# A gated feed-forward kernel behind pooled attention: a new opening, a plain end, GpSimd set aside earlier, next operands split first

## The chip, the cores and the metric

The kernel runs on one core of a Trainium2 chip. TensorE (PE) multiplies matrices, VectorE (DVE), ScalarE (ACT) and GpSimd (POOL) work on tiles, and SyncE (SP) issues the DMAs. The metric is the device time of one execution in microseconds (us), the median of several.

## The reference, cut to what matters

```python
# q, k, v: batch 8, heads 8, seq 576, head_dim 64;  w_a, w_b: 512 x 1536;  w_out: 1536 x 512
k_p = k.reshape(B, H, 72, 8, D).mean(axis=3)      # keys and values pooled by 8
v_p = v.reshape(B, H, 72, 8, D).mean(axis=3)
scores = q @ k_p.T / sqrt(D)
attn = exp(scores - max);  attn = attn / (attn.sum(-1) + 1e-9)
x = (attn @ v_p)            # laid out as 4608 tokens x 512
out = ((x @ w_a) * (x @ w_b)) @ w_out
```

The feed-forward weights reach the chip as 64-bit words and are turned into float32 there.

## The kernel before, in words

The 4608 tokens are 36 chunks of 128; three chunks make a half (384 tokens), two halves a pair, and there are six pairs. Every product is kept near float32 accuracy by parts: an operand is split into a high part (an fp32r copy, made by ScalarE) and a low part (the rest, a subtraction on VectorE or GpSimd), and one product is three matmuls, high by high, high by low and low by high.

A chunk passes through `chunk` (L797): its queries are split (L828), the scores are made on TensorE (`psc`, L913), VectorE subtracts the greatest score (L846, L847), ScalarE takes exponentials (L946), VectorE sums and inverts (L952, L953), the weights are divided (L958), split into high and low part `pr` and `rem` (L970, L972, L281) and turned on TensorE against an identity (`ptr`, L996): four turns for the high part, four for the low part, two for a remainder. ScalarE copies the turned parts out of PSUM (L1003). When the three chunks of a half are turned, `values_of` multiplies them by the pooled values (`po`, L1045 to L1048), and ScalarE and VectorE split the result into the operand tiles `xB`, `xT` (L1061, L281).

The feed-forward part runs over items. Items 0 to 7 are plain (`normal`, L1209 to L1211): 0 and 1 take the first half of pair 0, items 2 to 5 both halves, 6 and 7 the second half. From pair 1 on an item (`block`, L1352 to L1354) makes the inner products of a block of w_a and w_b by a scheme of seven products on sums and differences. Inner products gather in four PSUM banks `psXA`, `psXB`, `psYA`, `psYB`; the a and b parts are multiplied into gates `h`, which are split into `hh`. `outer` (L1427 to L1429) multiplies gates by w_out and adds to `y` in SBUF through two banks `acc` (L1489, L1492); from pair 2 on `outer_block` (L1459 to L1461) does it with seven products too, for which the gates are first combined (L1267) and w_out's sums are loaded from DRAM.

The order of the instructions is written by a planner while the program is built (`Machine`, with a rank for every task and an assumed cost for every operation). Elementwise work marked `either` goes to VectorE or GpSimd, whichever is free first in that plan, until the item number reaches `ALONE`. Each engine then runs its list strictly in order. Six PSUM banks serve the attention part while `psum["opening"]` holds; with the first inner product `close_opening` takes all four product banks away from it and two are left. Tiles with one buffer (`qh`, `ql`, `pr`, `rem`) or two (`weights`) make a chunk wait for an earlier one.

Of the kernel before, what the change touches and what calls it, by code (L numbers as in the profile page):

```python
# [9 lines left out]
F32 = mybir.dt.float32  # L10
# [75 lines left out]
SPARE = 1  # L86

ALONE = 8
# [13 lines left out]
NSLOT = 15  # L102

# [140 lines left out]
def attn_moe_kernel(ctx: ExitStack, tc: tile.TileContext, q, k, v, vr, wa, wb, wo, out):  # L244
# [86 lines left out]
    for item in items:  # L331
        due_item.append(t)
        t += 27.0 if item[0] == "s" else 13.0 * len(item[1])
# [17 lines left out]
    psum = {"free": ["att0", "att1", "XA", "XB", "YA", "YB"], "att": {"att0", "att1"}, "opening": True}  # L351
# [6 lines left out]
    def take_bank(name):  # L358
        tag = psum["free"].pop(0)
        return ps.tile([P, 512], F32, tag=tag, name=name), tag  # L360

    def give_bank(tag):
        if tag in psum["att"] or psum["opening"]:
# [18 lines left out]
    rawt.update({f: first_raw[:, f] for f in range(3)})  # L382
    spare = {n: sb.tile([P, 1536], I32, tag=f"x{t}", name=f"words_{n}", bufs=1) for n, t in zip("abo", ("T1", "T2", "T3"))}
# [20 lines left out]
    def convert_weights(name):  # L404
# [8 lines left out]
        for f in range(2):  # L413
            start(due_f[f] + delay - 6, load_words(f))
# [79 lines left out]
    def sums_outer():  # L494

        for j in range(NJ):
# [5 lines left out]
            kept["outer", j] = dr.tile([P, 2, 7, 2, P], F32, name=f"kept_outer_{j}")  # L502
# [29 lines left out]
            slots.give("rawo", j)  # L532

# [263 lines left out]
    def chunk(i, ready):  # L797
# [11 lines left out]
        yield until(("scores", i - 1))  # L809

        gap = P // 2 if len(parts) > 1 else 0
        qh = sb.tile([P, NK, P + P // 2], F32R, tag="qh", name=f"qh_{i}", bufs=1)
        ql = sb.tile([P, NK, P + P // 2], F32R, tag="ql", name=f"ql_{i}", bufs=1)
# [20 lines left out]
        yield until(("probs", i - 2))  # L834
# [3 lines left out]
        wide = weights[i % 2]  # L838
        s = wide[:, :, :SP]
        top = sb.tile([P, H], F32, tag="m", name=f"m_{i}")  # L840
        z = sb.tile([P, H], F32, tag="z", name=f"z_{i}")
# [60 lines left out]
        if i < SUMMED:  # L902
            for g0 in range(0, NK, 2):
                yield until(*(("keys", b, g0) for b, _, _ in by_batch))
                yield bank_there
                pt, tag = take_bank(f"psc_{i}_{g0}")
# [49 lines left out]
        yield either(  # L956
            H * SP,
            lambda eng: eng.tensor_tensor(  # L958
                out=s[:n], in0=s[:n], in1=z[:n].unsqueeze(2).broadcast_to([n, H, SP]), op=ALU.mult
            ),  # L960
        )
        mark("pooled", i)

        yield until(("turned", i - 1))
        pr = sb.tile([P, 2, H, KM], F32R, tag="pr", name=f"pr_{i}", bufs=1)
# [3 lines left out]
        def high():  # L969
            nc.scalar.copy(pr[:n, 0], s[:n, :, :KM])  # L970
# [3 lines left out]
        yield on_act(H * KM + 2 * H * KR, high, 3)  # L974

        def rest(eng):
            low_part(eng, pr[:n, 1], s[:n, :, :KM], pr[:n, 0])
            low_part(eng, rem[:n, :, 1], sr, rem[:n, :, 0])

        yield either(H * SP, rest, 2)  # L980
# [4 lines left out]
        if c0 == 0:  # L985
            yield until(("valued", half - 1))
            both = sb.tile([P, 2, NK, HB], F32R, tag="turned", name=f"turned_{half}", bufs=1)
            turned[half] = both[:, 0], both[:, 1], sb.tile([P, NG, HB], F32R, tag="rest", name=f"rest_{half}", bufs=1)

# [17 lines left out]
        for x in range(3):  # L1007
            yield bank_there
            pt, tag = take_bank(f"ptr_{i}_{x}")
# [11 lines left out]
    def values_of(j, rank):  # L1021
# [46 lines left out]
        for g0 in range(0, NK, per):  # L1068
            yield bank_there
            po, tag = take_bank(f"po_{j}_{g0}")  # L1070
# [12 lines left out]
    def prepare(p):  # L1083
# [20 lines left out]
        start(rank, split("B11", b11))  # L1104
        start(rank, combine(b11, b12, b11, "T1", ("operand", p, "B11")))
        start(rank + 1, split("B21", b21))
        start(rank + 2, combine(t2, b22, b11, "T2", ("T1", p)))
        start(rank + 3, split("T2", t2, ("T2", p)))
        start(rank + 4, split("T1", b11, ("T2", p)))
        start(rank + 5, combine(b12, b22, b12, "T3", ("T1", p)))  # L1110
        start(rank + 6, split("T3", b12, ("T3", p)))
        start(rank + 7, split("B22", b22, ("T2", p), ("T3", p)))
        start(rank + 8, combine(b21, b21, t2, "T4", ("T2", p), ("operand", p, "B21")))
        start(rank + 9, split("T4", b21, ("T4", p)))
# [490 lines left out]
```

## Time and profile before

| | before |
|---|---|
| runs, us | 998.48, 998.95, 999.3 (median 998.95) |
| profiled execution, us | 998.71, of which the profiled span is 996.9 |
| TensorE busy in the span | 960.7 us, 96% |
| VectorE, ScalarE, GpSimd busy | 867.9, 580.6, 83.3 us |

The span runs from the first instruction to the last; 1.8 us of the execution's time lie around it. A matmul's busy time overlaps with its neighbours', so the pace of TensorE is read from the distance of starts.

### The profile page before, as it was taken

The page shows a single profiled execution, that of the slowest core. Times are in us where ns is not written, and L with a number is a line of the kernel's source. Part 1 is how long each engine was busy: PE and PEld are TensorE (multiplying, and loading weights), DVE is VectorE, ACT ScalarE, POOL GpSimd, SP SyncE. Part 2 cuts the span into 40 slices and gives each one's busy share as a digit, 9 for nine tenths or more (in the row PEclk, how much of TensorE's full clock was granted, in tenths as well). Part 3 has the DMA queues.
Part 4 walks back from the last instruction along what each step waited for, and adds up shares of the span by engine and source line. Part 5 has one row for each costly group of instructions (what it writes and reads, how often), then busy time and mean ns, then how long its engine had stood idle before and what let it go on. Part 6 is the DMA issues. An engine that isn't in the chain of part 4 may idle for free.

```text
span 996.9 us, 16951 instructions
## 1 busy us (share of the span) xinstructions
PE 960.7 (96%) x5776; PEld 948.7 (95%) x5776; DVE 867.9 (87%) x1750; ACT 580.6 (58%) x1584; POOL 83.3 (8%) x93
## 2 busy tenths in 40 slices
PE   4689999999999999999999999999999999999997
PEld 3589999999999999999999999999999999999996
DVE  7987897589899999989899988989989889967777
ACT  4789897547766656674454584555475554443221
POOL 4331333161000000000000000000000000000000
PEclk9989999999999999999999999999999999999999
DMA  9768865566967878978857796876777666787661
GB/s 306 244 227 274 298 204 172 176 219 224 328 232 251 304 252 301 337 265 300 296 205 244 252 344 225 282 249 199 271 280 276 229 223 222 270 315 242 230 204 64
DMA packets 88342, 250.16 MB, mean 251 GB/s; under 512 B 9856, under 2 KB 17536, under 8 KB 88256
## 3 DMA queue, kind: packets, MB, share of 16 engines
q1 hardware_dynamic: 88256, 249.08, 72.0%
q8 instruction: 46, 0.75, 0.3%
q14 instruction: 40, 0.33, 0.1%
HBM read 197.13 MB, written 51.90 MB: 250 GB/s over the span
## 4 chain that ended last, share of the span: by engine, by line
PE 89%; DVE 7%; ACT 1%; issue 1%; DVEq 0%; ACTq 0%
PE acc L1459 6%; PE acc L1461 6%; PE acc L1460 6%; PE psc L913 5%; PE psXB L1352 4%; PE psXA L1352 4%; PE psXA L1354 4%; PE psXB L1353 4%; PE psXB L1354 4%; PE psXA L1353 4%; PE psYA L1352 3%; PE psYB L1352 3%; PE psYA L1354 3%; PE psYA L1353 3%; PE psYB L1354 3%; PE psYB L1353 3%
## 5 line engine op out<-in xcount | busy, mean ns | idle before, releaser
L1492 DVE TENSOR_TENSOR y<-acc,y 128x384 f32<-128x384 f32 x304 | 164.9, 553 | 27.9 <-PE acc L1461 23.4
L1259 ACT CAST hh<-h 128x384 fp32r<-128x384 f32 x168 | 85.1, 516 | 90.7 <-DVE h L1397 48.7
L281 DVE TENSOR_TENSOR hh<-h,hh 128x384 fp32r<-128x384 f32 x212 | 114.7, 558 | 5.0 <-ACT hh L1306 2.3
L1459 PE MATMUL acc<-hh,wo 128*128 128x384 f32 x336 | 116.5, 347 | 1.2 <-DVE y L1492 1.0
L1460 PE MATMUL acc<-hh,wo 128*128 128x384 f32 x336 | 113.9, 339 | 1.6 <-DVE hh L281 1.6
L1461 PE MATMUL acc<-hh,wo 128*128 128x384 f32 x336 | 113.7, 338 | 0.0
L1379 ACT COPY h<-psXA 128x384 f32<-128x384 f32 x90 | 43.2, 480 | 80.1 <-PE psXA L1354 79.7
L875 ACT ACTIVATE weights<-psc,least 128x72 f32<-128x72 f32 x240 | 74.0, 332 | 20.2 <-DVE least L891 19.7
L913 PE MATMUL psc<-kdiag,qh 128*128 128x144 f32 x320 | 59.3, 286 | 11.8 <-ACT kdiag L653 10.7
L1459 PEld LDWEIGHTS acc<-hh,wo 128*128 128x128 f32 x336 | 63.4, 189 | 3.8 <-DVE y L1492 3.5
L913 PEld LDWEIGHTS psc<-kdiag,qh 128*128 128x128 f32 x320 | 54.4, 204 | 12.6 <-issue 8.3
L1460 PEld LDWEIGHTS acc<-hh,wo 128*128 128x128 f32 x336 | 63.7, 190 | 2.2 <-DVE hh L281 2.2
L1461 PEld LDWEIGHTS acc<-hh,wo 128*128 128x128 f32 x336 | 63.5, 189 | 0.0
L1267 DVE TENSOR_TENSOR h<-h,h 128x384 f32<-128x384 f32 x96 | 52.9, 551 | 0.6
L1003 ACT CAST turned<-ptr 128x512 fp32r<-128x512 f32 x72 | 40.4, 592 | 21.3 <-PE ptr L996 21.1
L875 ACT ACTIVATION_READ_ACCUMULATOR weights<-psc,least 128x1 f32 x240 | 51.9, 216 | 0.0
L1397 DVE TENSOR_TENSOR h<-h,h 128x384 f32<-128x384 f32 x90 | 49.6, 551 | 0.4
L1352 PE MATMUL psXB<-xT,load 128*128 128x384 f32 x144 | 48.7, 338 | 0.0
L1352 PE MATMUL psXA<-xT,load 128*128 128x384 f32 x144 | 48.6, 337 | 0.0
L1353 PE MATMUL psXB<-xT,load 128*128 128x384 f32 x144 | 48.4, 336 | 0.0
L1353 PE MATMUL psXA<-xT,load 128*128 128x384 f32 x144 | 48.4, 336 | 0.0
L1354 PE MATMUL psXB<-xT,load 128*128 128x384 f32 x144 | 48.3, 336 | 0.0
(294 smaller groups left out, 3048.5 us busy)
## 6 DMA issues: line engine op xcount, KB each, us to landing
load<-kept_S SPq DMA_DIRECT2D x96, 512.0 KB, 5.0
load<-kept SPq DMA_DIRECT2D x72, 512.0 KB, 5.7
wo<-kept_outer SPq DMA_DIRECT2D x48, 512.0 KB, 4.3
wo<-kept_outer SPq DMA_DIRECT2D x48, 384.0 KB, 4.1
kept_S<-sum SPq DMA_DIRECT2D x24, 512.0 KB, 2.9
kept_outer<-osum SPq DMA_DIRECT2D x36, 256.0 KB, 3.7
out<-y SPq DMA_DIRECT2D x48, 192.0 KB, 2.1
kept<-sum SPq DMA_DIRECT2D x18, 512.0 KB, 6.4
```

Source lines behind the costliest of these rows:

```text
L281: eng.tensor_tensor(out=lo, in0=src, in1=hi.bitcast(F32), op=ALU.subtract)
L875: nc.scalar.activation(s[:n, h], src[:, h - hs.start], AF.Exp, bias=least[:n, h:h + 1], scale=SCALE, accum_out=z[:n, h:h + 1],)
L913: nc.tensor.matmul(pt[:n, j * hk:(j + 1) * hk], qq[:, g, cs], kd[:, g, w].rearrange("p e s -> p (e s)"), start=(x == 0), stop=(x == len(to ...
L1259: yield on_act(HB, lambda: nc.scalar.copy(e[:, 0], gf[item, src]))
L1267: yield either(HB, lambda eng: eng.tensor_tensor(out=t, in0=ta, in1=tb, op=ALU.subtract))
L1352: nc.tensor.matmul(pt, w[:, 0, mat, c], xo[:, 0, kk], start=(opens and kk == 0), stop=False, **more)
L1353: nc.tensor.matmul(pt, w[:, 0, mat, c], xo[:, 1, kk], start=False, stop=False, **more)
L1354: nc.tensor.matmul(pt, w[:, 1, mat, c], xo[:, 0, kk], start=False, stop=(kk == 1), **more)
L1459: nc.tensor.matmul(pt, w[:, 0], e[:, 0], start=opens, stop=False, **more)
L1460: nc.tensor.matmul(pt, w[:, 0], e[:, 1], start=False, stop=False, **more)
L1461: nc.tensor.matmul(pt, w[:, 1], e[:, 0], start=False, stop=True, **more)
L1492: yield on_dve(HB, lambda: nc.vector.tensor_tensor(out=acc[at], in0=pt, in1=acc[at], op=ALU.add))
```

## The change

Opening: the queries of chunk 1 get a tile of their own (`early_q`), chunk 2 gets a third `weights` tile, and the two of them no longer wait for the chunk before. For the first six chunks (`WHOLE`) the divided weights stay float32 in `pr` and are turned once, four turns instead of eight; high and low part are made from the turned result by ScalarE and VectorE. The four product banks are taken from the attention part one by one (`close`), and items 0 and 1 use the X banks alone. The first weight words are loaded at an earlier rank (`WORDS_RANK`), the first two items are due 6 us sooner, and chunks of pair 1 may not start before item 2.

End: the outer products of the last item are plain (`outer_last`): sixteen products in place of fourteen, from the gates themselves, without combining them; the results gather in eight banks. One more block of w_out is prepared for it (`left_plain`).

GpSimd: `ALONE` goes from 8 to 4. Next operands: in `prepare` the splits of a pair's operands get the rank -999.5.

```diff
-ALONE = 8
+SPLIT_RANK = -999.5
+ALONE = 4
...
+SOONER = 6.0
+WHOLE = PER_HALF * 2
+WORDS_RANK = 34.0
+WORDS_FIRST = 1
...
-        due_item.append(t)
+        due_item.append(t - (SOONER if len(due_item) < LEAD else 0.0))
...
-    def close_opening():
-        psum["opening"] = False
-        for tag in readable:
-            readable[tag] = tag in psum["free"]
-        psum["free"] = [x for x in psum["free"] if x in psum["att"]]
+    def close(tag):
+        psum["open"].remove(tag)
+        readable[tag] = tag in psum["free"]
+        if readable[tag]:
+            psum["free"].remove(tag)
...
+    early_x = sb.tile([P, 2, NK, P + P // 2], F32R, tag="xB22", name="early_q", bufs=1)
+    third = sb.tile([P, H, SP + 1], F32, tag="xT4", name="weights_2", bufs=1)
...
-            start(due_f[f] + delay - 6, load_words(f))
+            start(WORDS_RANK if f < WORDS_FIRST and name != "o" else due_f[f] + delay - 6, load_words(f))
...
-        yield until(("scores", i - 1))
+        yield until(("scores", i - 2 if 0 < i < 3 else i - 1))
...
-        yield until(("probs", i - 2))
+        if i != 2:
+            yield until(("probs", i - 2))
...
-        wide = weights[i % 2]
+        wide = third if i == 2 else weights[i % 2]
...
+        if whole:
+            yield until(("turned", i - 1))
+            pr = sb.tile([P, H, KM], F32, tag="pr", name=f"pr_{i}", bufs=1)
+            def divide_both(eng):
+                divide(eng, s[:n, :, KM:], s[:n, :, KM:])
+                divide(eng, pr[:n], s[:n, :, :KM])
+            yield either(H * SP, divide_both, 2)
...
+        def turn_whole(pt):
+            for g in range(NK):
+                src = pr[:n, 2 * g:2 * g + 2, :].rearrange("p a s -> p (a s)")
+                nc.tensor.transpose(pt[:, g * P:g * P + n], src, ident[:n, :n].bitcast(F32))
+        def take_whole(pt, tag):
+            yield m.SETTLE
+            src = pt.rearrange("p (g s) -> p g s", g=NK)[:, :, :n]
+            hi, lo = (turned[half][x][:, :, c0:c0 + n] for x in range(2))
+            yield on_act(NK * n, lambda: nc.scalar.copy(hi, src))
+            yield on_dve(NK * n, lambda: low_part(nc.vector, lo, src, hi))
...
-        start(rank + 3, split("T2", t2, ("T2", p)))
+        start(SPLIT_RANK, split("T2", t2, ("T2", p)))
...
-                    bank = ("X", "Y")[u if len(us) > 1 else y] + "AB"[mat]
+                    bank = ("X", "Y")[u if len(us) > 1 else y if u else 0] + "AB"[mat]
...
+        if item == items[-1]:
+            for name, what in (("B11", "C11"), ("B22", "C22"), ("B12", "C12"), ("B21", "C21")):
+                start(rank, split(name, what, what))
+                start(rank, leave(what, "split " + name))
+            return
...
+    def outer_last(item, x0):
+        a11, a12, a21, a22 = 0, 5, 7, 6
+        first = [("C11", a11), ("C21", a21)]
+        steps = [(0, *x, "B11", True, False) for x in first]
+        for c in range(2):
+            for what, l1, l2 in (("C12", a11, a12), ("C22", a21, a22)):
+                steps += [(c, what, l1, "B12", True, False), (c, what, l2, "B22", False, True)]
+        steps += [(1, *x, "B11", True, False) for x in first]
+        steps += [(c, what, left, "B21", False, True) for c in range(2) for what, left in (("C11", a12), ("C21", a22))]
...
+            def products():
+                nc.tensor.matmul(pt, w[:, 0], e[:, 0], start=opens, stop=False)
+                nc.tensor.matmul(pt, w[:, 0], e[:, 1], start=False, stop=False)
+                nc.tensor.matmul(pt, w[:, 1], e[:, 0], start=False, stop=ends)
...
+            if p == 1:
+                x = max(x, LEAD)
```

TensorE, from the turning of chunk 2 to the first values product. Before (`ptr` turns, `psc` scores, `po` values product):

```order
L996 MATMUL ptr_0_343<-ident,pr_321 128x128 x4
L996 MATMUL ptr_1_349<-ident,pr_321 128x128 x4
L996 MATMUL ptr_2_354<-ident,rem_322 96x128 x2
L913 MATMUL psc_0_365<-kdiag_72,qh_336 128x144 x2
L913 MATMUL psc_0_365<-kdiag_72,ql_337 128x144
L913 MATMUL psc_0_365<-kdiag_72,qh_336 128x144 x2
L913 MATMUL psc_0_365<-kdiag_72,ql_337 128x144
L913 MATMUL psc_2_375<-kdiag_72,qh_336 128x144 x2
L913 MATMUL psc_2_375<-kdiag_72,ql_337 128x144
L913 MATMUL psc_2_375<-kdiag_72,qh_336 128x144 x2
L913 MATMUL psc_2_375<-kdiag_72,ql_337 128x144
L1045 MATMUL po_0_386<-turned_229,vdiag_74 128x384
```

TensorE at the same place now, from the turning of chunk 0 (L1045 is the float32 turn):

```order
L1045 MATMUL ptr_0_259<-ident,pr_230 128x128 x4
L1063 MATMUL ptr_2_268<-ident,rem_243 96x128 x2
L1045 MATMUL ptr_0_289<-ident,pr_271 128x128 x4
L1063 MATMUL ptr_2_298<-ident,rem_278 96x128 x2
L1045 MATMUL ptr_0_320<-ident,pr_301 128x128 x4
L1063 MATMUL ptr_2_329<-ident,rem_308 96x128 x2
L1117 MATMUL po_0_344<-turned_257,vdiag_74 128x384
L1118 MATMUL po_0_344<-turned_257,vdiag_74 128x384
```

The scores of chunk 3 stood ahead of the values product and now stand behind the first twenty-four inner products; the scores of chunks 0 to 2 all stand ahead of the first turn, and four turns of each chunk are gone.

VectorE, from the row after chunk 2's inverse sum to the division of its weights (`weights_81`, `pr_301`), as it stands now:

```order
L287 TENSOR_TENSOR rem_243<-weights_77,rem_243 128x2x32
L287 TENSOR_TENSOR own_21_252<-raw_first,own_21_252 128x512
L768 TENSOR_REDUCE vp_171<-early_9_95 96x64
L998 TENSOR_TENSOR weights_78<-weights_78,z_152 128x8x8
L998 TENSOR_TENSOR pr_271<-weights_78,z_152 128x512
L768 TENSOR_REDUCE vp_171<-early_9_95 96x64
L287 TENSOR_TENSOR turned_257<-ptr_0_259,turned_257 128x4x128
L287 TENSOR_TENSOR rem_278<-weights_78,rem_278 128x2x32
L798 SCALAR_TENSOR_TENSOR kv_5_294<-vp_171,mask 96x256 x2
L998 TENSOR_TENSOR weights_81<-weights_81,z_212 128x8x8
L998 TENSOR_TENSOR pr_301<-weights_81,z_212 128x512
```

Before, one row (`vrem`) stood between that inverse and the division of chunk 2; the work of chunks 0 and 1 that now stands there came ahead of chunk 2's exponentials.

TensorE at the end of the program, from the middle of the last inner product (`psXB`) on. Before:

```order
L1354 MATMUL psXB_5_0_11564<-xT_5_10552,load_466_11557 128x384
L1352 MATMUL psXB_5_0_11564<-xT_5_10552,load_466_11557 128x384
L1353 MATMUL psXB_5_0_11564<-xT_5_10552,load_466_11557 128x384
L1354 MATMUL psXB_5_0_11564<-xT_5_10552,load_466_11557 128x384
L1459 MATMUL acc_5_0_1_11771<-hh_187_11758,wo_469_11655 128x384
L1460 MATMUL acc_5_0_1_11771<-hh_187_11758,wo_469_11655 128x384
L1461 MATMUL acc_5_0_1_11771<-hh_187_11758,wo_469_11655 128x384
L1459 MATMUL acc_5_0_0_11743<-hh_190_11768,wo_468_11654 128x384
```

Now:

```order
L1433 MATMUL psXB_5_0_11538<-xT_5_10486,load_480_11531 128x384
L1591 MATMUL acc_5_0_C_11733<-hh_481_11601,wo_482_11628 128x384
L1592 MATMUL acc_5_0_C_11733<-hh_481_11601,wo_482_11628 128x384
L1593 MATMUL acc_5_0_C_11733<-hh_481_11601,wo_482_11628 128x384
L1591 MATMUL acc_5_0_C_11737<-hh_481_11601,wo_483_11629 128x384
L1592 MATMUL acc_5_0_C_11737<-hh_481_11601,wo_483_11629 128x384
L1593 MATMUL acc_5_0_C_11737<-hh_481_11601,wo_483_11629 128x384
L1591 MATMUL acc_5_0_C_11741<-hh_174_11726,wo_482_11628 128x384
```

All 48 matmuls of the last outer products now stand behind the last inner product; before, 3 of 42 stood ahead of it. The first six work on a gate (`hh_481`) that is made two products earlier.

## Rows read from the trace of the kernel before

**Rows 1.** The page: TensorE's busy time, and its tenths in 40 slices.

```profile
PE 960.7 (96%) x5776; PEld 948.7 (95%) x5776; DVE 867.9 (87%) x1750; ACT 580.6 (58%) x1584; POOL 83.3 (8%) x93
PE   4689999999999999999999999999999999999997
```

**Rows 2.** Windows: length, busy us of each engine, granted clock, DMA share, GB/s.

```profile
30.00:40.00 10.00, 4.86 (x23) 4.27 (x24) 9.29 (x14) 8.29 (x19) 4.20 (x5) 1.00 0.76 254
120.00:160.00 40.00, 40.00 (x249) 39.84 (x248) 33.89 (x65) 38.45 (x115) 13.79 (x14) 1.00 0.53 178
130.00:230.00 100.00, 100.00 (x608) 99.66 (x606) 75.52 (x140) 67.25 (x199) 40.39 (x38) 1.00 0.54 184
300.00:500.00 200.00, 199.18 (x1222) 197.80 (x1221) 186.13 (x395) 124.01 (x363) 0.57 (x2) 1.00 0.81 287
980.00:997.00 17.00, 10.82 (x41) 7.45 (x39) 11.24 (x22) 2.00 (x4) 0.00 (x0) 0.90 0.26 93
```

**Rows 3.** Timeline of TensorE's opening: start, us, line, tiles, [idle before].

```profile
13.55 0.41 PE L913 MATMUL psc<-kdiag,ql 128*128 128x144 f32 x1
...
33.71 0.75 PE L996 MATMUL ptr<-ident,pr 128*128 128x128 f32 x4 [4.75 <-ACT pr L970]
...
39.76 0.61 PE L1045 MATMUL po<-turned,vdiag 128*128 128x384 f32 x1
...
45.02 0.45 PE L1209 MATMUL psXA<-xB,own 128*128 128x384 f32 x1 [1.28 <-DVE xB L281]
...
47.23 0.34 PE L913 MATMUL psc<-kdiag,qh 128*128 128x144 f32 x2
...
49.87 0.38 PE L1209 MATMUL psXB<-xB,own 128*128 128x384 f32 x1
50.09 0.34 PE L1210 MATMUL psXB<-xB,own 128*128 128x384 f32 x1
...
52.02 0.80 PE L996 MATMUL ptr<-ident,pr 128*128 128x128 f32 x8
...
60.31 0.51 PE L996 MATMUL ptr<-ident,pr 128*128 128x128 f32 x4 [1.67 <-DVE weights L847]
...
64.29 0.42 PE L996 MATMUL ptr<-ident,rem 128*96 128x128 f32 x2 [0.77 <-ACT turned L1003]
...
64.95 0.52 PE L1428 MATMUL acc_n<-hh,wo 128*128 128x384 f32 x1
65.27 0.52 PE L1429 MATMUL acc_n<-hh,wo 128*128 128x384 f32 x1
```

**Rows 4.** Timeline of the other engines in the opening.

```profile
27.84 0.68 ACT L946 ACTIVATE weights<-weights 128x576 f32<-128x576 f32 x1
...
35.67 1.28 POOL L281 TENSOR_TENSOR own<-raw_first,own 128x512 fp32r<-128x512 f32 x1 [0.48 <-ACT own L454]
...
36.14 1.35 DVE L281 TENSOR_TENSOR ql<-q,qh 128x512 fp32r<-128x512 f32 x1 [0.56 <-ACT qh L828]
37.42 0.68 DVE L441 SCALAR_TENSOR_TENSOR raw_first<-raw_first,words_a 128x512 int32<-128x512 int32 x1
```

**Rows 5.** Groups by shape, 130 to 230 us: instructions, busy us, mean ns.

```profile
L281 POOL TENSOR_TENSOR own<-raw,own 128x512 fp32r<-128x512 f32 x5 | 6.7, 1332 | 27.2 <-ACT own L488 16.0 <-ACT own L454 9.1 <-PE acc_n L1429 2.2
L281 DVE TENSOR_TENSOR own<-raw,own 128x512 fp32r<-128x512 f32 x11 | 9.9, 911 | 0.0
```

**Rows 6.** TensorE's waits from 250 to 400 us: what waited for what, us, times, longest.

```profile
PE po L1045 <- ACT weights L875: 0.8, 1, 0.8
```

**Rows 7.** Timeline of the end.

```profile
979.92 0.34 PE L1354 MATMUL psXB<-xT,load 128*128 128x384 f32 x1
980.10 0.38 PE L1459 MATMUL acc<-hh,wo 128*128 128x384 f32 x1
...
993.28 0.34 PE L1461 MATMUL acc<-hh,wo 128*128 128x384 f32 x1
993.66 0.56 DVE L1492 TENSOR_TENSOR y<-acc,y 128x384 f32<-128x384 f32 x1 [0.21 <-PE acc L1461]
```

More of the change, by code (lines that the diff above doesn't have):

```diff
@@ L356, in bank_there, with later_bank_there, take_bank @@
         return bool(psum["free"])
-    def take_bank(name):
-        tag = psum["free"].pop(0)
+    def later_bank_there():
+        return any(x not in ("XA", "XB") for x in psum["free"])
+    def take_bank(name, later=False):
+        tag = [x for x in psum["free"] if not later or x not in ("XA", "XB")][0]
+        psum["free"].remove(tag)
         return ps.tile([P, 512], F32, tag=tag, name=name), tag
     def give_bank(tag):
-        if tag in psum["att"] or psum["opening"]:
+        if tag in psum["att"] or tag in psum["open"]:
             psum["free"].append(tag)
@@ L532, in sums_outer, with left_plain @@
             slots.give("rawo", j)
+    def left_plain():
+        j = NJ - 1
+        yield until(("kept", "outer", j, 3))
+        yield lambda: at_item[0] >= items.index(("s", NPAIR - 2, 0)) and slots.can("osum")()
+        e = slots.take("osum", (j, 7), [P, 2, 2, 2, P], F32R)[:, :, :1]
+        yield tmps.can("o")
+        w = tmps.take("o", "left", tmp_shape, F32)
+        yield transfer(w, kept["raw o", 2 * j], 1 << 18)
+        by = w[:, 256:].rearrange("p (o c s) -> p c o s", o=1, c=2)
+        yield on_act(256, lambda: [nc.scalar.copy(e[:, c, :, 0], by[:, c]) for c in range(2)], 2)
+        yield either(256, lambda eng: [low_part(eng, e[:, c, :, 1], by[:, c], e[:, c, :, 0]) for c in range(2)], 2)
+        tmps.give("o", "left")
+        for c in range(2):
+            dst = kept["outer", j][:, c, 7:8].rearrange("p o l s -> p (o l s)")
+            yield transfer(dst, e[:, c].rearrange("p o l s -> p (o l s)").bitcast(F32), 1 << 17)
+        mark("kept", "outer", j, 7)
+        slots.give("osum", (j, 7))
     def spare_for(kind):
@@ L1005, in take_turned @@
             mark("placed", i, x)
-        for x in range(3):
-            yield bank_there
-            pt, tag = take_bank(f"ptr_{i}_{x}")
+        if whole:
+            yield later_bank_there if i >= PER_HALF else bank_there
+            pt, tag = take_bank(f"ptr_{i}_0", i >= PER_HALF)
+            yield on_pe(NK * 0.21, lambda: turn_whole(pt))
+            start(rank, take_whole(pt, tag))
+        for x in range(2 if whole else 0, 3):
+            yield later_bank_there if i >= PER_HALF else bank_there
+            pt, tag = take_bank(f"ptr_{i}_{x}", i >= PER_HALF)
             yield on_pe(mms(NK if x < 2 else NG, n), lambda: turn(x, pt))
@@ L1131, in attn_moe_kernel @@
         if kind == "s" and item[1] >= 2:
-            order_o += [(j, c, x) for c in range(2) for x in range(2)]
+            order_o += [(j, c, x, 4 if item == items[-1] else 4 - x) for c in range(2) for x in range(2)]
         else:
@@ L1177, in there @@
         def there():
-            if psum["opening"]:
-                close_opening()
+            if bank in psum["open"]:
+                close(bank)
             return readable[bank]
@@ L1405, in outer @@
             kind, p, j = item
+            if item == items[-1]:
+                yield from outer_last(item, x)
+                continue
             if kind == "s" and p >= 2:
@@ L1439, in outer @@
                         opens, closes = j == LEAD, j == LEAD - 1
-                    start(TOP + 1, taken_outer(p if kind == "s" else 0, half, c, bank, pt, opens, closes))
+                    start(TOP + 1, taken_outer(p if kind == "s" else 0, half, c, (acc_free, bank), pt, opens, closes))
     def outer_block(item, x0):
@@ L1496, in taken_outer @@
             yield MARGIN
-        acc_free[bank] = True
+        if isinstance(bank, str):
+            give_bank(bank)
+        else:
+            bank[0][bank[1]] = True
         if closes:
@@ L1548, in attn_moe_kernel @@
         start(SUMS_RANK, sums_outer())
+        start(SUMS_RANK, left_plain())
         start(1e3, load_parts())
```

108 lines of the change are left out of this document (74 added, 34 removed).

## The prediction, made before the changed kernel was run

> **What bounds the kernel now.** I read the page first. TensorE is busy in 96% of the span, and its tenths show where it is not: the first four slices and the last [rows 1]. The windows say the same of the middle: from 300 to 500 us TensorE lacks 0.8 us of 200, with VectorE at 93% (186.1 of 200) [rows 2]. So the middle is TensorE's own work, and a change can win only at both ends, or lose in the middle by making TensorE wait. The timelines of the ends came next, as idle time and pace. The pace: twelve 384-column matmuls run from 49.87 to 52.02, so 0.18 us each (the last eleven 0.175); twenty-four 144-column ones from 47.23 to 49.87, so 0.11 each [rows 3]. The spacing of 0.32 us at 64.95 is TensorE at its lower clock, 1.2 GHz, after the gaps ahead of it; 0.175 is 2.4 GHz.
>
> In the opening the first inner product starts at 45.02 us, though only 94 matmuls stand ahead of it: 48 of 144 columns, 30 turns and 16 of 384, about 11 us of work at the fast pace. After it TensorE still idles in four gaps from 60.31 to 64.29 (1.67 the first, 0.77 the last, 3.6 together) and then runs nine wide matmuls and eight of half the width at the low clock [rows 3], which costs 9 x 0.145 + 8 x 0.11 = 2.2 us. What holds it is a chain through VectorE, which is busy in 9.29 of 10 us there [rows 2].
>
> At the end the last inner product ends near 980.1 and the last matmul starts at 993.28 [rows 7]: 13.4 us for 39 matmuls that need 6.8, so 6.5 us are waits and slow clock (granted clock 0.90 in that window [rows 2]).
>
> **The opening, step by step.** Chunk 0's scores end at 13.96 in the old kernel (13.55 + 0.41 [rows 3]). Now chunks 1 and 2 need no tile of the chunk before, so their 24 matmuls follow at once; at the low clock 0.22 each, 5.3 us, to 19.3. VectorE's greatest and difference, and the older rows of its list, I put at 2.1 us: chunk 2's exponentials start near 21.4 and not at 27.84 [rows 4]. They take 0.68. Then VectorE has the sum, the inverse and the twelve instructions shown in the order: seven of 512 columns or so at 0.68 [rows 4] and seven small ones that I put at 0.27 each, 6.7 us, so chunk 2's division is done at 28.8; the old kernel turned that chunk at 33.71 [rows 3]. Four turns at the low clock, 0.75 for the old ones [rows 3], 1.5 if a float32 turn costs two of those; the copy behind four conversions on ScalarE about 2 us. The values product starts near 32.5 and not at 39.76, because chunk 3's scores no longer stand between. From there to the first inner product it was 5.3 us, on the same rows, and I keep that: 37.8, I take 38. That is 7.0 us earlier, of which chunk 3's 12 scores, done later now, take back 1.3: 5.7.
>
> After that start the new order has 72 inner products (12.7 us) with one chunk's scores between, ahead of the next turn, where the old one had gaps worth 3.6 + 2.2 = 5.8. The X banks alone serve them, so each must be read out before it opens again; I allow 2 us of such waits. Gain 3.8. Opening in all: 9.5 us. The bounds are 4 (only half of the chain shortens, the gaps move later) and 13 (nothing waits).
>
> Edits that I cost at nothing. The earlier weight words: two loads of 512 KB go ahead of batch 1's keys, which come about 4 us later at 254 GB/s [rows 2]; the next thing that needs those keys, chunk 4's scores, stands behind the 72 inner products. If that cover were gone it would cost those 4 us. The float32 turn: 24 of them replace 48, eight of which took 0.80 with the last one's end [rows 3]. No row has a float32 matmul. Between the same price each (0.10, a gain of 2.4 us) and two 384-column matmuls (0.35, a loss of 3.6) I take 0.20, the pair it replaces, the nearest row: nothing. The later chunks of pair 1 and the bank rule change what is ready, not how much is done.
>
> The Trainium skill, "FP8 and Floating Point Precision" (TensorE Precision Notes), says that true float32 goes through the array in four passes. By that a turn costs 0.40 and the sum would be 4.8 us higher; no row here shows it.
>
> **The end.** The last item no longer combines gates, and 48 matmuls replace 42. Three of the old ones ran before the inner product's end, so that end comes 0.5 earlier, at 979.6. 48 x 0.175 = 8.4. The first six work on a gate made two products earlier and cover 1.05 us of splitting; the next gate's low part stands behind the last product's VectorE row, and I allow 0.4. Last matmul done at 988.4 in place of 993.5: 5.1. Behind it one addition (0.56 [rows 7]) and a store as before; the eight stores now come closer together, 0.3. Gain 4.8, between 2 (half of the waits come back) and 6 (no wait, old tail).
>
> **GpSimd off from item 4, and the split rank.** From 130 to 230 us GpSimd runs 38 instructions, 40.4 us [rows 2]. At VectorE's price, 0.68 for 512 columns [rows 4] against 1.33 on GpSimd [rows 5], that is 20.6 us. VectorE gets some time back: its own 512-wide rows took 0.911 there and 0.68 alone, 11 times, 2.5 us [rows 5]. So 75.5 + 20.6 - 2.5 = 93.6 of 100 us, as from 300 to 500, where TensorE lost 0.8 in 200. I take a loss of 1.0. The bounds: a gain of 0.8, the longest wait that the middle now has [rows 6], and a loss of 20.6. The splits of the next operands move ahead of gates and additions in two engines that keep TensorE fed; the old middle has no wait at a change of pair, so I cost it at nothing, inside the same bounds.
>
> VectorE's 1.35 us at 36.14 stands beside GpSimd's 35.67 to 36.95, and the same width takes 0.68 alone [rows 4]. The Trainium skill, "SBUF — State Buffer" (Who interferes with whom), has a rule for it: the two share a port pair under an exclusive lock for the whole instruction. By that rule GpSimd's new work in the opening, chunk 1's low part and chunk 0's division, would hold VectorE up once each, 0.7 us a time, and the sum would be 1.3 higher; the trace agrees with the lock.
>
> **The sum.** Against the profiled execution: 998.7 - 9.5 - 4.8 + 1.0 = 985.4. Its time is 0.2 under the median of the runs, so 985.6; I say 985.5.
>
> **The rivals.** *ScalarE keeps the pace.* From 120 to 160 us it is busy in 38.45 of 40 us [rows 2]; a TensorE that is 9.5 us ahead wants its rows sooner. The change takes from ScalarE one 512-wide copy and one 512-wide read per chunk, 12 x 0.5 = 6 us for six chunks. If the lead shrinks to that, 3.5 us come back: 989. For it: that window. Against: the list was also idle early, and TensorE had no wait there.
>
> *The lead is lost wholly.* The float32 turning takes no wide subtraction from VectorE, it only moves it behind the turn, and VectorE is 93% busy. If its list is the bound all through the opening, the first inner product comes earlier but the gaps return behind it. Then only the end remains: 998.9 - 4.8 + 1.0 = 995.1. Against: the order has 72 inner products ready.
>
> *Slower: VectorE becomes the bound.* The place is 130 to 230 us, the price GpSimd's 20.6. It decides once VectorE's 24.5 idle us there cannot be used, because its rows come in bunches behind TensorE's banks: TensorE then waits for gates and additions. With both ends' gains the time is 998.9 - 14.3 + 20.6 = 1005. Against: 93% from 300 to 500 at hardly any cost.
>
> **How the numbers follow.** Forecast 0.62 (981 to 988.5); ScalarE 0.20 (987 to 993); lead lost 0.08 (993 to 997); slower 0.08 (1001 to 1008); the rest, 0.02, is an offset of gains and losses within 0.2%, about 2 us, which is what a measurement of this kernel can tell from no change. The range 980 to 993 leaves out the last three and the forecast's lower edge, under 2 in 10. Faster 0.90, same 0.02, slower 0.08.
>
> **What would show it.** Right: the first inner product at 38 +- 2 us, no gap over 1 us between it and 70 us and no low clock there; from the end of the last inner product to the last matmul's end under 9.5 us; TensorE short of less than 4 us from 100 to 970. Wrong: the first inner product after 41 us; gaps behind it that ScalarE or VectorE ends; waits for `h`, `hh` or `y` between 130 and 300; turns of chunks 0 to 5 well over 0.8 us for four at the fast clock.

## The result and the profile after

The changed kernel takes 981.4 us (median of 981.18, 981.36, 981.44 and 984.44) against 998.72 for the kernel before in the same comparison: ratio 0.9831, 95% interval 0.9813 to 0.9848. The forecast was 985.5 in 980 to 993. Executions of one kernel differ by up to 4.5 us, mostly with TensorE's granted clock: some have low stretches, at 1.2 GHz in place of 2.4, most often between 60 and 100 us (mean of an execution 0.991 to 1.000); where that matters, spans at a mean clock of 1.0 are compared, which is called equal clock below. The profiled execution of the changed kernel, 984.44 us, is the one of the four that has such stretches.

The page: busy time, and TensorE's tenths, to be read beside [rows 1].

```profile
PE 954.3 (97%) x5758; PEld 945.3 (96%) x5758; DVE 864.8 (88%) x1779; ACT 574.0 (58%) x1571; POOL 44.6 (5%) x60
PE   4799999999999999999999999999999999999998
```

Only the first two slices and the last are under nine tenths now; before, the first three and the last were. GpSimd lost 39 us of work, and VectorE is no busier than before (867.9 in [rows 1]). The windows, as in [rows 2]:

```profile
40.00:70.00 30.00, 28.10 (x182) 27.15 (x181) 28.30 (x58) 26.13 (x56) 11.04 (x12) 1.00 0.74 257
70.00:100.00 30.00, 28.12 (x169) 27.58 (x168) 24.26 (x50) 27.15 (x78) 5.31 (x5) 0.89 0.82 266
130.00:230.00 100.00, 100.00 (x603) 99.54 (x602) 84.48 (x175) 65.37 (x188) 0.56 (x2) 1.00 0.58 199
```

From 130 to 230 us VectorE is busy for 84.5 us. I had worked out 93.6 for it. The opening on the other engines, to be read beside [rows 4]:

```profile
21.08 0.68 ACT L984 ACTIVATE weights<-weights 128x576 f32<-128x576 f32 x1 [1.12 <-DVE weights L885]
...
27.84 0.67 DVE L998 TENSOR_TENSOR pr<-weights,z 128x512 f32<-128x512 f32 x1
...
32.74 0.68 DVE L287 TENSOR_TENSOR turned<-ptr,turned 128x512 fp32r<-128x512 f32 x1
```

These are chunk 2's exponentials, its division and the low part of its turned weights. TensorE's opening, beside [rows 3]:

```profile
28.57 1.12 PE L1045 MATMUL ptr<-ident,pr 128*128 128x128 f32 x4 [0.90 <-DVE pr L998]
...
32.23 0.69 PE L1117 MATMUL po<-turned,vdiag 128*128 128x384 f32 x1 [2.01 <-ACT turned L1051]
33.48 0.69 PE L1118 MATMUL po<-turned,vdiag 128*128 128x384 f32 x1 [0.56 <-DVE turned L287]
...
36.84 0.48 PE L1120 MATMUL po<-rest,vrem 96*128 96x384 f32 x1
...
39.38 0.44 PE L1283 MATMUL psXA<-xB,own 128*128 128x384 f32 x1 [1.36 <-DVE xB L287]
...
69.68 0.36 PE L1118 MATMUL po<-turned,vdiag 128*128 128x192 f32 x1 [1.46 <-DVE turned L287]
...
73.07 0.52 PE L1510 MATMUL acc_n<-hh,wo 128*128 128x384 f32 x1
73.39 0.52 PE L1511 MATMUL acc_n<-hh,wo 128*128 128x384 f32 x1
...
90.75 0.54 PE L1063 MATMUL ptr<-ident,pr 128*128 128x128 f32 x4 [1.53 <-ACT weights L913]
```

The row at 28.57 is the float32 turn of chunk 2, still at the low clock. The first inner product starts 5.6 us earlier than in [rows 3]. No wait over 0.1 us follows it up to 63 us; then the gaps are back, 1.46 and 1.53 us the longest, and the spacing of 0.32 at 73.07 is the low clock. The end, beside [rows 7]:

```profile
970.01 0.34 PE L1433 MATMUL psXB<-xT,load 128*128 128x384 f32 x1
970.19 0.33 PE L1591 MATMUL acc_C<-hh,wo 128*128 128x384 f32 x1
...
971.54 0.44 PE L1592 MATMUL acc_C<-hh,wo 128*128 128x384 f32 x1
...
978.69 0.34 PE L1593 MATMUL acc_C<-hh,wo 128*128 128x384 f32 x1
```

The 48 matmuls run through, with one hold of 0.11 us at 971.54. And TensorE's waits from 100 to 970 us (what waited for what: us in all, times, longest) are one row, where the kernel before had four, 1.9 us in all:

```profile
PE psXB L1431 <- DVE h L1464: 0.5, 2, 0.3
```

### The profile page after: what moved, and what is told of

The parts are those of the page before. It is cut to its first block, busy times and chain, and to the rows that moved or that the text cites. A ratio compares the mean times of both kernels' runs of the same rounds, so it can differ in the third digit from the quotient of the medians.

```text
span 982.6 us, 16941 instructions
## 1 busy us (share of the span) xinstructions
PE 954.3 (97%) x5758; PEld 945.3 (96%) x5758; DVE 864.8 (88%) x1779; ACT 574.0 (58%) x1571; POOL 44.6 (5%) x60
## 4 chain that ended last, share of the span: by engine, by line
PE 93%; DVE 4%; ACT 1%; issue 1%; DMA 1%; SPq 0%; POOL 0%; DVEq 0%; ACTq 0%
PE acc L1541 6%; PE acc L1543 6%; PE acc L1542 6%; PE psc L951 5%; PE psXB L1431 4%; PE psXB L1433 4%; PE psXA L1431 4%; PE psXB L1432 4%; PE psXA L1432 4%; PE psXA L1433 4%; PE psYB L1431 3%; PE psYA L1431 3%; PE psYB L1433 3%; PE psYA L1432 3%; PE psYA L1433 3%; PE psYB L1432 3%
## 5 line engine op out<-in xcount | busy, mean ns | idle before, releaser
L1619 DVE TENSOR_TENSOR y<-acc,y 128x384 f32<-128x384 f32 x290 | 157.1, 552 | 25.6 <-PE acc L1543 17.0
L1333 ACT CAST hh<-h 128x384 fp32r<-128x384 f32 x165 | 83.0, 516 | 78.9 <-DVE h L1476 41.8
L1541 PE MATMUL acc<-hh,wo 128*128 128x384 f32 x322 | 110.0, 342 | 0.0
L1542 PE MATMUL acc<-hh,wo 128*128 128x384 f32 x322 | 108.3, 336 | 0.0
L1543 PE MATMUL acc<-hh,wo 128*128 128x384 f32 x322 | 108.3, 336 | 0.0
L951 PE MATMUL psc<-kdiag,qh 128*128 128x144 f32 x312 | 55.4, 277 | 9.3 <-ACT kdiag L687 8.5
L951 PEld LDWEIGHTS psc<-kdiag,qh 128*128 128x128 f32 x312 | 51.7, 197 | 9.7 <-issue 8.0
L1542 PEld LDWEIGHTS acc<-hh,wo 128*128 128x128 f32 x322 | 60.5, 188 | 0.0
L1541 PEld LDWEIGHTS acc<-hh,wo 128*128 128x128 f32 x322 | 60.5, 188 | 0.0
L1543 PEld LDWEIGHTS acc<-hh,wo 128*128 128x128 f32 x322 | 60.4, 188 | 0.0
L1341 DVE TENSOR_TENSOR h<-h,h 128x384 f32<-128x384 f32 x92 | 50.5, 549 | 0.5
L1476 DVE TENSOR_TENSOR h<-h,h 128x384 f32<-128x384 f32 x90 | 49.4, 549 | 0.3
L1431 PE MATMUL psXA<-xT,load 128*128 128x384 f32 x144 | 48.7, 338 | 0.0
L1432 PE MATMUL psXA<-xT,load 128*128 128x384 f32 x144 | 48.4, 336 | 0.0
L1433 PE MATMUL psXA<-xT,load 128*128 128x384 f32 x144 | 48.3, 336 | 0.0
```

The source lines that it names most:

```text
L951: nc.tensor.matmul(pt[:n, j * hk:(j + 1) * hk], qq[:, g, cs], kd[:, g, w].rearrange("p e s -> p (e s)"), start=(x == 0), stop=(x == len(to ...
L1333: yield on_act(HB, lambda: nc.scalar.copy(e[:, 0], gf[item, src]))
L1341: yield either(HB, lambda eng: eng.tensor_tensor(out=t, in0=ta, in1=tb, op=ALU.subtract))
L1431: nc.tensor.matmul(pt, w[:, 0, mat, c], xo[:, 0, kk], start=(opens and kk == 0), stop=False, **more)
L1432: nc.tensor.matmul(pt, w[:, 0, mat, c], xo[:, 1, kk], start=False, stop=False, **more)
L1433: nc.tensor.matmul(pt, w[:, 1, mat, c], xo[:, 0, kk], start=False, stop=(kk == 1), **more)
```

## The experiments

Each was timed beside the kernel before, whose median was 999.0 to 999.3 in these comparisons.

### Does the sum divide as forecast? The opening alone, and the opening with the end

The opening alone: the changed kernel without `outer_last` and `left_plain`, with

```diff
-ALONE = 4
+ALONE = 8
-        start(SPLIT_RANK, split("B11", b11))
+        start(rank, split("B11", b11))
...
-            order_o += [(j, c, x, 4 if item == items[-1] else 4 - x) for c in range(2) for x in range(2)]
+            order_o += [(j, c, x, 4 - x) for c in range(2) for x in range(2)]
```

> The changed kernel's opening with the old end, the old ranks of the splits and GpSimd up to the eighth item. My prediction's term (9.5 us): 989.6. Theory A (the rest of the 17.3 us, when the end's 4.8 and 4.5 for the middle are taken away, is the opening's): 991. Theory B (an earlier opening runs into GpSimd's and the splits' waits in the middle, so that part of its gain is given back there): 993 to 996, with waits between 200 and 420 us of 4 us or more.

989.02 us, ratio 0.9894 (0.9881 to 0.9908): about 10 us, as forecast (9.5). Its windows behind the start of the inner products, and then the first of these windows of the kernel before:

```profile
40.00:70.00 30.00, 28.09 (x182) 27.15 (x181) 28.19 (x57) 26.17 (x56) 11.00 (x12) 1.00 0.74 255
70.00:100.00 30.00, 27.98 (x189) 27.43 (x189) 26.39 (x54) 29.35 (x84) 5.36 (x5) 1.00 0.87 283
```

```profile
40.00:70.00 30.00, 25.16 (x149) 24.08 (x149) 26.12 (x52) 23.98 (x58) 12.46 (x14) 0.89 0.61 198
```

The clock is full in both of its windows. In the kernel before a mean of 0.89 over 30 us is 3.3 us of full clock not granted; TensorE idles for part of that stretch, so its matmuls lose 2.5 to 3 us by it. So the middle edits are not needed for the opening's gain, and theory B (given back in the middle) fell: TensorE's waits from 100 to 970 us are 1.8 us here. Theory A, 991, was 2 us too high. Which of the opening's edits gave what is not shown: but for the turning, below, none was taken back by itself.

With the plain end added, the middle edits alone put back:

```diff
-ALONE = 4
+ALONE = 8
...
-        start(SPLIT_RANK, split("B11", b11))
+        start(rank, split("B11", b11))
```

> The changed kernel with both middle edits put back: GpSimd works up to the eighth item and the splits have their old ranks; the new opening and the plain end stay. Theory A (the two middle edits are worth the sum of what each cost when put back alone, 4.7 and about 3 us): 988 to 989. Theory B (each only moves a wait that the other creates or removes; the opening alone gave 989.0 and the end is worth 4.8 to 5): 984 to 985, so that both together are worth about 3. My prediction's term (a loss of 1.0): 980.4.

984.9 us, ratio 0.9857 (0.9844 to 0.9871). So the end is worth 4.1 on the opening, and the two middle edits together 3.5 more; at equal clock (spans 982.4 and 983.4 against 979.4 to 979.7) it is 3 to 4. That is theory B's number. My term for them was a loss of 1.0. TensorE's waits from 100 to 970 us here:

```profile
PE acc_s L1510 <- DVE hh L287: 0.8, 1, 0.8
PE ptr L1063 <- DVE rem L287: 0.6, 1, 0.6
PE psXA L1433 <- DVE sum L287: 0.4, 1, 0.4
```

### The end taken back

```diff
-            if item == items[-1]:
-                yield from outer_last(item, x)
-                continue
...
-        start(SUMS_RANK, left_plain())
```

> The changed kernel with the old end: the last item combines its gates again, 42 matmuls in place of 48. Theory A (the plain end's gain is the waits between the last inner product and the last matmul, worked out at 4.8 us): 986.2, and 13 to 14 us from the end of the last inner product to the last matmul's end. Theory B (the old end's waits came from the late state of VectorE in the old middle and are gone without the plain end too): 982 to 984.

988.91 us, ratio 0.9893 (0.9879 to 0.9907). Four of its five executions have the low stretch and one has not: that one takes 986.2, theory A's number, with a span of 984.4 us against 979.4 to 979.7, so the end is worth 4.8 at equal clock. The waits are those of the kernel before; first two of them here, then the longest of the kernel before:

```profile
972.79 0.44 PE L1534 MATMUL acc<-hh,wo 128*128 128x384 f32 x1 [1.44 <-DVE hh L287]
...
978.70 0.44 PE L1533 MATMUL acc<-hh,wo 128*128 128x384 f32 x1 [0.65 <-DVE y L1611]
```

```profile
981.91 0.44 PE L1460 MATMUL acc<-hh,wo 128*128 128x384 f32 x1 [1.44 <-DVE hh L281]
```

Theory B (the old end's waits go without the plain end too) fell.

### The middle edits, one at a time, on the changed kernel

GpSimd back to the eighth item:

```diff
-ALONE = 4
+ALONE = 8
```

> The changed kernel with one number put back: GpSimd works up to the eighth item again and not only up to the fourth. Theory A (what TensorE lacked between 200 and 970 us in the kernel before came from the pair GpSimd and VectorE holding each other up, and the early end of GpSimd's work took it away): about 985 us, 3 to 4.5 above the changed kernel's 981.4, and waits between 200 and 420 us of 3 us or more. Theory B (the earlier splits of the next operands took it away): 980.5 to 982.5. Theory C (my prediction's term: GpSimd's absence costs 1 us): 980.4.

986.4 us, ratio 0.9874 (0.9861 to 0.9888): 5.0 more. Its two longest waits from 100 to 970 us:

```profile
PE psYA L1283 <- ACT own L503: 1.0, 1, 1.0
PE psYA L1285 <- DVE own L287: 0.8, 1, 0.8
```

They come at 221 to 223 us, for weights that ScalarE and VectorE split late. With a third of 0.5 us for `y` they are 2.3 us, not theory A's 3 or more; all waits from 100 to 970 us are 2.8 us, against 0.5 in the changed kernel. So waits are about half of the 5.0, and the rest is not assigned to a row. VectorE's rows for them and for the sums of w_out by shape from 130 to 230 us (busy us, mean ns), with GpSimd at work:

```profile
L287 DVE TENSOR_TENSOR osum<-rawo,osum 128x256 fp32r<-128x256 f32 x10 | 6.5, 690 | 3.5 <-ACT osum L525 3.3
L287 DVE TENSOR_TENSOR own<-raw,own 128x512 fp32r<-128x512 f32 x8 | 6.1, 760 | 0.2 <-issue 0.2
```

and in the changed kernel, with GpSimd idle:

```profile
L287 DVE TENSOR_TENSOR own<-raw,own 128x512 fp32r<-128x512 f32 x14 | 9.6, 684 | 0.4 <-ACT own L469 0.4
L287 DVE TENSOR_TENSOR osum<-rawo,osum 128x256 fp32r<-128x256 f32 x12 | 4.5, 419 | 1.3 <-ACT osum L525 1.3
```

The old ranks of the splits, with GpSimd off from the fourth item:

```diff
-        start(SPLIT_RANK, split("B11", b11))
+        start(rank, split("B11", b11))
```

(and so for the other six splits).

> The changed kernel with the old ranks of the seven splits of the next pair's operands. Theory A (GpSimd's absence is the gain of the middle): 980.5 to 982.5. Theory B (the ranks are): 984.5 to 986, with waits at the changes of pair, which come near 245, 430, 610 and 790 us. My prediction's term for the ranks was nothing.

985.36 us, ratio 0.9862 (0.9848 to 0.9875): 4.0 more at the median, near 3 at equal clock (982.4 at 0.999 against 979.6 at 1.0). Its two longest waits, at 392.80 and 398.60 us, are at the change of pair, for the operands whose splits are late again; all waits from 100 to 970 us are 1.7 us:

```profile
PE psXA L1432 <- DVE xB L287: 1.0, 1, 1.0
PE psXA L1432 <- DVE xT L287: 0.5, 1, 0.5
```

With neither edit the kernel takes 984.9, with the ranks alone 986.4, with GpSimd off alone 985.4, with both 981.4. So neither of theories A and B is right by itself: each edit alone gains nothing, and only the two together do. The intervals of the first three overlap; that of the last, 0.9813 to 0.9848, just reaches the nearest of them (0.9844), and its spans at equal clock, 979.4 to 979.7, lie 2.7 us or more under every span of the other three.

### The middle edits on the kernel before

GpSimd up to the fourth item only:

```diff
-ALONE = 8
+ALONE = 4
```

> The kernel before with one number changed: GpSimd works up to the fourth item and not up to the eighth. Theory A (GpSimd and VectorE hold each other up, so the waits between 240 and 400 us, 2.3 us in the kernel before, go): about 997 us. Theory B (without the earlier splits the waits only move to the change of pair near 390 us, as in the changed kernel with the old ranks): 998.5 to 1000. My prediction's term: 1000.

1000.22 us, ratio 1.0006 (0.9997 to 1.0015). The waits at 244 to 255 us went, and 1.6 us of waits came at 391 to 404 us, two of them again for `xB` and `xT`. These are theory B's waits, with a median 0.2 us over its range. My term's 1.0 is met by chance: the interval holds no change at all, and the waits are at a place that the term did not have. With the early splits as well:

```diff
-ALONE = 8
+ALONE = 4
...
-        start(rank, split("B11", b11))
+        start(-999.5, split("B11", b11))
```

> The kernel before with both middle edits, GpSimd up to the fourth item and the early splits of the next operands. Theory A (each alone moves the waits, both together take them away): 996 to 997, and no wait over 0.3 us between 110 and 970. Rival (the middle's gain in the changed kernel rests on its opening, which ends earlier): no change, 998.5 to 999.5. My prediction's term: 1000.

1004.6 us, ratio 1.0053 (1.004 to 1.0065), slower by 5.3: every expectation missed. The waits at 390 us are gone, but the largest stand at 550 to 556 us, the next change of pair:

```profile
PE acc L1459 <- DVE y L1492: 2.3, 2, 1.6
PE psXA L1353 <- DVE xT L281: 1.2, 1, 1.2
```

```profile
540.00:560.00 20.00, 16.47 (x79) 14.99 (x78) 19.49 (x35) 9.15 (x17) 0.00 (x0) 0.86 0.70 247
```

79 matmul records lie in these 20 us and 126 in the changed kernel's, with VectorE full (19.5 of 20) in both and the clock down to 0.86 behind the waits (0.89 from 540 to 570 us, 3.3 us of full clock not granted). The waits, 4.4 us in all, are 2.5 more than in the kernel before, so waits and clock together make up the 5.3. The same two edits gain 3.5 us behind the new opening and lose 5.3 behind the old one.

### The turning

```diff
-WHOLE = PER_HALF * 2
+WHOLE = 0
```

> The changed kernel with the old turning: the weights of the first six chunks are again split into two parts and turned twice each, 48 turns in place of 24; the early pieces keep their own tiles. Theory A (a float32 turn costs one fp32r turn, as the changed kernel's trace has it, 0.37 us for four at the fast clock, and what is saved is half of the turns and ScalarE's and VectorE's rows ahead of the first inner product): 984 to 986, first inner product 1 to 2 us later than 39.4. Theory B (the turning is only moved, the tiles alone make the opening earlier): 981 to 982. Theory C (fewer gaps between 60 and 100 us, because VectorE's wide subtraction stands ahead of the turn again): 979.

993.47 us, ratio 0.9944 (0.9931 to 0.9956): 12 us more at the median and 10 between the two profiled executions, both at a mean clock of 0.997; far outside all three expectations. The first inner product came earlier, at 38.03 us, not later. The waits from 100 to 970 us grew to 3.9 us, the two longest:

```profile
PE psXA L1432 <- DVE xT L287: 1.4, 1, 1.4
PE psXA L1432 <- DVE xB L287: 0.6, 1, 0.6
```

The new list again brings waits near 240 us and at the change of pair near 400 us, and from the first inner product to 100 us it has 5.7 us of them against 3.8. So the waits are some 5 of the 10 us. The turns themselves explain little of it, as the next four kernels show; the rest is not assigned. They turn more chunks in float32: all 36, from the nineteenth on, from the thirteenth on, and, after these, from the twenty-fifth on (beside the first six).

```diff
-        whole = i < WHOLE
+        whole = i < WHOLE or i >= 24
...
-            yield on_pe(NK * 0.21, lambda: turn_whole(pt))
+            yield on_pe(NK * (0.21 if i < WHOLE else 0.095), lambda: turn_whole(pt))
```

with 18 and 12 in place of 24; for all chunks `WHOLE = NCHUNK` and 0.095.

> The changed kernel with the float32 turning for all 36 chunks in place of the first six (and its price in the planner's list put at the measured one, 0.095 us a turn). Theory A (four float32 turns take 0.37 us where eight fp32r ones take 0.80; TensorE bounds the middle, so 30 chunks by 0.43 us come off it): 968 to 970. Theory B (the subtraction behind the turn makes VectorE late, and TensorE waits for it): 975 to 985. Theory C (a float32 turn costs two fp32r ones and the trace shows only their starts): 981 and no fewer us of TensorE's work.

> The changed kernel with the float32 turning for the first six chunks and from the nineteenth on, the twelve between turned as before. Theory A (behind 430 us TensorE has no waits and VectorE keeps up, so 18 chunks by 0.43 us come off): 973 to 975. Theory B (VectorE, 88% busy, does not keep up with a TensorE that is 7.7 us faster there; the waits that the kernel with all chunks turned in float32 showed come back later): 978 to 982.

> The changed kernel with the float32 turning for the first six chunks and from the thirteenth on. Theory A (24 chunks by 0.43 us): 971 to 973. Theory B (the waits of 378 to 398 us, at the next pair's operands, appear as in the kernel with all chunks in float32, about 4.5 us): 976 to 978, and slower than with the float32 turning from the nineteenth on.

> The changed kernel with the float32 turning for the first six chunks and for the last twelve, the eighteen between turned as before. Theory A (the wait of 3.3 us between 540 and 555 us that took part of the gain in the kernel from the nineteenth chunk on belongs to the chunks turned ahead of it, and is not there now; 12 chunks by 0.43 us come off TensorE's work): 976 to 977. Theory B (a TensorE that is faster by anything runs into a wait of about 3 us at a later change of pair, near 600 or 730 us): 979 to 980.

All chunks: 984.41 us (0.9842, 0.9829 to 0.9856), with 7 us of waits from 100 to 970 us. From the nineteenth: 979.85 (0.9810, 0.9797 to 0.9824). From the thirteenth: 979.76 (0.9814, 0.9798 to 0.9830). From the twenty-fifth: 981.33 (0.9816, 0.9800 to 0.9832), all its executions at a mean clock of 0.997 or 0.998. Theory A, 0.43 us a chunk, fell in all four. Theory B's number holds for all chunks and from the nineteenth. From the thirteenth it missed by 2 us, with the longest waits near 550 us and not at 378 to 398, and from the twenty-fifth on neither theory holds: no wait of 3 us came. The price of the turns, from the last of these kernels, eight fp32r turns and what follows, then four float32 ones:

```profile
344.97 0.80 PE L1063 MATMUL ptr<-ident,pr 128*128 128x128 f32 x8
345.61 0.41 PE L1431 MATMUL psYB<-xT,sum 128*128 128x384 f32 x1
...
583.35 0.60 PE L1045 MATMUL ptr<-ident,pr 128*128 128x128 f32 x4
583.71 0.36 PE L1063 MATMUL ptr<-ident,rem 128*96 128x128 f32 x2
583.91 0.40 PE L1541 MATMUL acc<-hh,wo 128*128 128x384 f32 x1
```

Eight fp32r turns take 0.64 from start to the next start and four float32 ones 0.36; the pair behind them takes 0.20 in place of the usual 0.12. By these rows a chunk saves 0.2 us, not the 0.43 of the expectations, which had taken the busy time of a group (0.80) for its pace. From the first matmul on `acc` to the last inner product the kernel from the twenty-fifth on takes 568.15 us and the changed kernel 571.43: 3.3 us for 12 chunks, 0.27 each, of which 0.02 is a shorter wait; one wait of 0.2 us is left from 100 to 970. From the nineteenth on a part is lost at the change of pair at 550 us:

```profile
PE acc L1541 <- DVE y L1619: 1.7, 2, 1.4
PE psXA L1432 <- DVE xT L287: 0.4, 1, 0.4
```

At a mean clock of 1.0 that kernel's spans are 977.6 to 978.1 (and one of 980.2), 1.3 to 2.1 us under the changed kernel's. By the intervals of the ratios it isn't told apart from it, and no kernel tried beats it surely.

## Why the prediction was right or wrong

**The opening, 9.5 forecast, about 10 measured: right in size, in part by luck, and its chain right up to the values product.** Forecast and measured: chunk 2's exponentials 21.4 and 21.08; its division done 28.8 and 28.51; the values product 32.5 and 32.23. Ahead of the exponentials two errors cancel: chunk 2's scores end at 20.06 and not at 19.3, and VectorE needs 1.0 us behind them and not 2.1. The step that failed is "From there to the first inner product it was 5.3 us, and I keep that": it is 7.15. The second product waits until 33.48 for the low part that VectorE makes at 32.74, behind the turn and no longer ahead of it; in the old kernel the second product came 0.41 us after the first. And the low clock, spacing 0.32, lasts to 36.84, over twelve products against six before. So the lead is 5.6 us and, less chunk 3's scores (1.3), worth 4.3 and not 5.7.

Behind the start I had 3.8 us for gaps that go; this step failed too. The gaps did not go: 0.34, 1.46, 1.53 and 0.35 us in the changed kernel, 3.7 in all, against 4.1. They moved behind 63 us, as my rival of the lost lead said of them, and they are what I had named as a sign of being wrong. Only the clock came back, 2.5 to 3 us, in those executions where it stays up. The float32 turns, costed at nothing, give 3 x 0.27 = 0.8 us for chunks 3 to 5; those of chunks 0 to 2 are part of the lead. Together 4.3 + 2.5 to 3 + 0.4 + 0.8 is 8.0 to 8.5, so 1.5 to 2 us of the 10 are not assigned. That the sum came out at 9.5 is in part luck: the lead was 1.4 us too large, the 3.8 us were nearly met by the clock and not by gaps, and the rest lay in no term. (The slices under nine tenths in [rows 1] are the first three, not four; nothing hangs on it.)

Here the Trainium skill, "FP8 and Floating Point Precision" (TensorE Precision Notes), with its four passes for true float32, would have made the sum worse by 4.8 us. The measured float32 turns of a group start 0.11 us apart at 2.4 GHz, fp32r ones 0.08, so the measurement decides against using the rule for a turn. At 1.2 GHz, where chunks 0 to 2 are turned, it is 0.21 against 0.13: four float32 turns show 1.12 us there, at 28.57, and four fp32r ones 0.75, at 33.71 in [rows 3].

**The end, 4.8 forecast: right.** From the start of the last inner product to the last matmul's end it is 9.02 us against 13.70, a gain of 4.7; taken back it costs 4.8 at equal clock, and added to the opening alone it gives 4.1. What follows the last matmul takes 3.6 us and was 3.3, the 0.3 I had added.

**The middle, a loss of 1.0 forecast, a gain of 3 to 4 measured: wrong in sign.** The step that failed is "75.5 + 20.6 - 2.5 = 93.6". GpSimd's 40 us became only 9 more on VectorE, 84.5. The work did move: GpSimd has 36 instructions fewer there and VectorE 35 more (175 against 140). What I undersized is the 2.5 us that VectorE's own rows give back; by the windows it is 75.5 + 20.6 - 84.5 = 11.6. I had counted one kind of row, `own`, 911 ns in [rows 5] and 684 now, but others were stretched while GpSimd ran. By shape, a small row of the attention part and the combining of w_out's blocks, in the kernel before and in the changed one:

```profile
L891 DVE TENSOR_SCALAR least<-m 128x4 f32<-128x4 f32 x7 | 3.3, 473 | 0.2
L529 DVE TENSOR_TENSOR rawo<-rawo 128x256 f32<-128x256 f32 x5 | 3.2, 637 | 0.0
```

```profile
L929 DVE TENSOR_SCALAR least<-m 128x4 f32<-128x4 f32 x7 | 1.2, 170 | 0.2
L544 DVE TENSOR_TENSOR rawo<-rawo 128x256 f32<-128x256 f32 x12 | 4.9, 412 | 0.1
```

Taken shape by shape at the lengths of the changed kernel, the 36 rows that left GpSimd are 20.3 us on VectorE, so that price was right, and VectorE's own rows of the kernel before are 9.2 us shorter: `own` 2.5, `least` 2.1, `rawo`, `rem` and `xraw` 1.1 each, the rest 1.3. What is left of the 11.6 is not assigned; the two windows do not hold quite the same rows.

The Trainium skill, "SBUF — State Buffer" (Who interferes with whom), has the two engines share a port pair under an exclusive lock, and these rows agree; the runs show the longer rows and not the lock itself. That the idle time on VectorE is what gained is argued from here: shown is that GpSimd's return costs 5 us, of which 2.3 are waits for rows of ScalarE and VectorE. Nor did my "cost it at nothing" for the split rank hold: with GpSimd off the waits move to the change of pair near 390 us, and the early splits take those away.

That the same edits lose 5.3 us behind the old opening shows what my sum could not hold: in a written order most of the waits sit near the changes of pair (about 240, 390 and 550 us), and an edit anywhere ahead moves them. VectorE has little idle time there (in the kernel before it is busy for 19.5 of 20 us from 240 to 260, 13.5 of 15 from 385 to 400, 19.9 of 20 from 540 to 560), but it is as busy from 680 to 720, 39.4 of 40, where no wait in any of these traces is over 0.3 us; so a full VectorE alone does not make them. On the new opening and end 0.5 us of waits from 100 to 970 us went with 981.4, and 1.7 to 2.8 us with 984.9 to 986.4; on the old ones 1.6 to 1.9 us with 999 to 1000, and 4.4 us with 1004.6. Why the list of the changed kernel has none at any of the three, and that of its neighbours one or two, is not settled: the waits show it, no single edit explains it.

**The rivals.** ScalarE did not keep the pace where I had placed it: no wait over 0.1 us from 100 to 970 us ends with it. Up to 100 us three of the four gaps end with it, 0.34, 1.53 and 0.35 us. The lead was not lost. The 1.3 us that the lock between VectorE and GpSimd was to cost in the opening did not come: VectorE's rows beside GpSimd's new ones, at 9.18 and from 18.64 to 19.95, take 0.20 to 0.72 us, as the same rows do elsewhere. Only beside GpSimd's split of weights, from 23.62 to 25.10, is one longer, 0.69 us at 24.49 and 0.21 at 27.70. VectorE became the bound nowhere in the changed kernel; on the old opening the two edits did reach the rival's 1005, but at 550 us and not from 130 to 230, and by 3.5 us of waits in one place and the low clock behind them.

## What to carry to other kernels

A chain priced by its rows came out here to a few tenths at each main point, though two errors inside it cancelled; but work moved behind a turn (here VectorE's low part) is late for the step after it, so follow it one step further. When work moves off an engine that slows its neighbour, take back the stretch from all of the neighbour's rows, not from one kind. And in a planned order try edits in combination, and look at the waits where one group of operands gives way to the next: the same two edits won 3.5 us in one order and lost 5.3 in another.

## What the runs showed of the hardware

A float32 turn of 128 by 128 against an identity takes 1.3 times as long as an fp32r one at 2.4 GHz, 0.109 us from start to start within a group against 0.084, and 1.7 times at 1.2 GHz, 0.213 against 0.127. Four of them are so cheaper than eight fp32r ones at either clock: 0.36 us, and 0.08 more on the pair behind them, against 0.64 at the fast clock.

After one and the same gap the granted clock sometimes falls and sometimes does not. In the changed kernel's profiled execution the matmuls behind the 1.46 us gap at 69.68 ran at a spacing of 0.32 us at 73.07; with GpSimd back to the eighth item nearly the same gap came, and 0.17 to 0.18 us behind it:

```profile
69.60 0.36 PE L1118 MATMUL po<-turned,vdiag 128*128 128x192 f32 x1 [1.44 <-DVE turned L287]
...
72.16 0.34 PE L1510 MATMUL acc_n<-hh,wo 128*128 128x384 f32 x1
72.33 0.34 PE L1511 MATMUL acc_n<-hh,wo 128*128 128x384 f32 x1
```

So about 3 us of an execution hang on whether the clock stays at 2.4 GHz there and behind the gap of 1.53 us at 90.75, and a comparison of kernels by 1 to 3 us has to look at the clock first.
